# Sorted block attention into a gated MLP: the second batch's attention output turned by transposing transfers, all units in a new order, the last copy on two engines

## The chip, the core and the metric

The kernel runs on one core of a Trainium2 chip. The core has a matrix engine (TensorE, PE in the profile), a vector engine (VectorE, DVE), a scalar engine (ScalarE, ACT), a general engine (GpSimd, POOL) and a sequencer for transfers (SyncE, SP). SP, ACT and POOL issue transfers, which 16 DMA engines carry out. TensorE writes only to PSUM, eight banks of 128 partitions by 2 KB; VectorE and ScalarE copy results from there to the on-chip memory SBUF. The metric is the device time of one execution in microseconds; the median of several runs counts.

## The reference

Inputs are q, k, v (4 batches, 8 heads, 768 tokens, 64 per head) and sort_net (4, 8, 8, 8), and four weights of an MLP. First sorted block attention:

```python
P = sort_net
for _ in range(5):                       # Sinkhorn
    P = np.exp(P - np.max(P, axis=-1, keepdims=True))
    P = P / (np.sum(P, axis=-1, keepdims=True) + 1e-09)
    P = P / (np.sum(P, axis=-2, keepdims=True) + 1e-09)
k_sorted = np.einsum('bhij,bhjcd->bhicd', P, k_b)   # 8 blocks of 96 tokens, mixed by P
v_sorted = np.einsum('bhij,bhjcd->bhicd', P, v_b)
scores = scale * q_b @ k_sb.T            # each block attends to its own mixed block
attn = softmax(scores)
attn_out = attn @ v_sb                   # -> x: (4, 768, 512)
```

then a gated MLP with a spatial mix over the 768 tokens:

```python
h = np.maximum(x @ w_in, 0.0)            # 512 -> 1024
u, v = h[..., :512], h[..., 512:]
v_n = (v - mean) / sqrt(var + 1e-06)     # over the 512
v_s = np.einsum('ts,bsd->btd', w_spatial, v_n) + b_spatial[None, :, None]
out = (u * v_s) @ w_out                  # (4, 768, 512)
```

## The kernel before

Everything is cut into units, small functions `u_XX`, and one written list (`ORDER`) says in which order they are issued. An item such as `VP:14:D:0:3` calls `u_VP` with its arguments. Each engine works off its own instructions in the order in which the list issues them, and waits where a tile that it needs is not ready or a buffer not free; so the list sets the order on PE, DVE, ACT, POOL and on the queues of SP and ACT alike. Nothing is planned at run time.

PSUM is addressed by a number, the first argument of most units: 0 to 3 are pairs of banks, 10 to 17 the single banks, so 0 holds 10 and 11, 1 holds 12 and 13, 2 holds 14 and 15, 3 holds 16 and 17. A letter (A or D) names the engine that copies the result out. Then come the batch and the part of it: a head pair hp (four of them), a half ih of the blocks (two), a tile n of 128 tokens (six), a chunk mc of 128 gate columns (four).

The units, in the order in which a batch passes through them:

- `SK` (five times, at the start, for all batches): one Sinkhorn step on ACT and DVE; `PR`, `P0`, `PC`, `PD`: the mixing matrices pd, by PE and DVE for batch 0, by POOL for the others.
- `L`: a load, issued by POOL, which also casts to bf16; `LH`, `QC`: half of batch 0's q, loaded by ACT's queue as it is and cast on ACT.
- `QT` (and `QQ`, two head pairs at once): q turned on PE by 12 transposes, L324. In batch 3 `QP` reorders q and `QX` turns it by a transposing transfer.
- `KT`, `VT`: k or v mixed by pd on PE and turned at once, L393. `VB` turns v back by blocks, L411. For batches 1 to 3 `VM` mixes v on PE (L420) and `VC` distributes it by eight transfers (L433), which AT reads as vb.
- `SC`: scores of one head pair and half, PE L452, and their exponential on ACT, L457.
- `AT`: the attention output, PE L498, divided by the sums on DVE, L505 and L506, into the tile x.
- `XT`: x turned for the MLP: eight transposes on PE (L528) and a copy out of PSUM for one half and two head pairs. `XD`: the same for one half and all head pairs by a transposing transfer from SP, L516. Before the change batches 0 and 1 use XT, four units each, and batches 2 and 3 use XD, two each.
- `VP`: the v half of the first MLP matrix for one or two token tiles, PE L564, with ReLU on the way out. `ST`: its mean and variance on DVE, L581 and L582; `LN`: the inverse root on ACT; `LA`: the normalising on DVE, L593. `WT` (and `WW`, two at once): the spatial weight turned on PE.
- `UP`: the u half, PE L607. `SP`: the spatial mix of one chunk, PE L619, plus the bias on DVE into z, L625; it needs all six normalised tiles of its batch. `GT`: u times z, on POOL or DVE. `OP`, `OE`, `OS`: the last product (L645), its copy and its store.
- For the end of batch 3 `SH`, `GH`, `OH`, `OI`, `OJ` do the last four with smaller pieces.
- `DM`: matmuls on zeros at the start, as many as the second number, so that PE works before its data arrive. `CK`, `CF`, `LF`: whether the sums stayed in range; the branch at `IF` would otherwise recompute all by a general path, which does not run here.

Batches overlap: while PE does the MLP of one batch, it does the attention of the next between.

Of the kernel before, what the change touches and what calls it, by code (L numbers as in the profile page):

```python
# [34 lines left out]
VP:10:D:1:3 SC:1:2:3:0 SC:3:2:1:0 ST:1:0 GT:P:0:1 ST:1:4 QP:A:3:2 ST:1:3 UP:2:A:1:0:1 OP:0:0:2:2 ST:1:5 AT:1:2:2:1  # L35
OE:A:0:2 AT:3:2:3:0 OP:2:0:0:2 LN:1:0:6 LA:1:0 LA:1:5 LA:1:1 QP:A:3:3 OE:A:0:0 OP:0:0:4:2 OE:A:0:4 LA:1:4 LA:1:3
VM:1:A:3:3 VM:3:A:3:1 QP:A:3:0 LA:1:2 SP:2:1:0 XD:2:1 QX:3:0:4 VM:0:A:3:2 AT:1:2:0:0 SP:3:1:1 L:k:3:0:8 VM:2:D:3:0
AT:0:2:1:0 SP:1:1:3 OS:0:2:0:2 UP:3:A:1:1:1 VC:3:0:4 AT:2:2:2:0 KT:0:A:3:0 KT:1:D:3:1 XD:2:0 GT:P:1:3 KT:3:D:3:2
GT:P:1:1 KT:2:A:3:3 SP:0:1:2 SC:1:3:2:0 SC:2:3:2:1 VP:16:A:2:5 AT:0:3:2:0 VP:17:D:2:3 SC:1:3:3:0 SC:2:3:0:1 OS:0:4:0:2
ST:2:3 ST:2:5 SC:0:3:1:1 VP:16:D:2:4 VC:3:4:8:0:4 AT:1:3:3:0 VP:17:A:2:0 UP:2:A:2:1:1 AT:0:3:2:1 VP:16:D:2:2 ST:2:2  # L40
SC:1:3:0:0 ST:2:0 GT:P:1:0 SC:2:3:1:0 SC:0:3:3:1 ST:2:4 VP:17:A:2:1 UP:1:A:2:1:0 ST:2:1 UP:2:A:2:0:0 GT:P:1:2 LN:2:0:6
AT:0:3:3:1 OP:3:1:2:2 OE:A:1:2 LA:2:4 LA:2:3 AT:1:3:0:0 AT:2:3:1:1 LA:2:5 LA:2:2 OP:0:1:4:2 AT:3:3:1:0 AT:1:3:0:1
UP:2:A:2:0:1 LA:2:1 LA:2:0 OP:3:1:0:2 OE:A:1:4 XD:3:0 OS:0:0:0:2 XD:3:1 SP:1:2:2 SP:2:2:3 GT:D:2:3 SP:0:2:1 CK
SP:1:2:0 VP:10:A:3:1 VP:11:A:3:2 OE:D:1:0 VP:14:A:3:5 ST:3:5 VP:10:A:3:0 GT:D:2:0 OS:1:0:0:2:A UP:1:D:3:0:1 CF:11
GT:P:2:1 VP:10:D:3:3 GT:P:2:2 ST:3:3 UP:3:D:3:1:0 ST:3:0 ST:3:1 VP:11:A:3:4 ST:3:4 ST:3:2 LF OP:2:2:2:2 LN:3:0:6
LA:3:1 LA:3:2 UP:1:A:3:0:0 OE:A:2:2 LA:3:5 LA:3:3 OP:3:2:0:2 LA:3:0 LA:3:4 OP:0:2:4:2 OE:D:2:0 UP:1:D:3:1:1 OE:A:2:4
OS:1:2:0:2 SH:14:3:2:0 SH:15:3:3:0 GH:P:3:3:0 SH:14:3:0:0 GH:D:3:2:0 SH:15:3:1:0 GH:P:3:0:0 SH:14:3:1:1 SH:12:3:2:1
OS:2:4 GH:P:3:1:0 SH:15:3:3:1 OS:2:0 GH:D:3:1:1 SH:14:3:0:1 OS:1:4 GH:D:3:3:1 OS:2:2 GH:P:3:0:1 GH:P:3:2:1 IF
# [788 lines left out]
```

## Time and profile before

| | |
|---|---|
| time, median of 3 runs | 153.27 us (153.04 to 153.84) |
| the profiled execution | 154.13 us, span 152.3 us |
| PE busy | 143.7 us (94%) |
| DVE busy | 114.7 us (75%) |
| ACT busy | 85.0 us (56%) |
| POOL busy | 42.3 us (28%) |
| instructions | 4112 |
| moved by DMA | 24.38 MB |

The span is the time from the first to the last instruction in the trace of one execution; the profiled execution's own time lies 1.8 us above it and 0.86 us above the median of the runs. Busy time of PE counts matmuls whose ends are modelled, since they are pipelined. A group in the profile is a line, an engine, an operation and its shapes, with the number of instructions, their busy time in us, the mean duration of one in ns, and the engine's idle time just before them with what ended it. The chain of waits is followed back from the last instruction, at each step to what released it, or to the instruction before it on its engine. L123 and L121 are a helper, `copy`, on DVE and on ACT; L129 and L127 the same for ReLU.

### The profile page before, as it was taken

What the parts mean: (1) busy time and instruction counts of PE and PEld (TensorE: products, weight loads), DVE (VectorE), ACT (ScalarE), POOL (GpSimd) and SP (SyncE); (2) the same over time, 40 slices, a digit from 0 to 9 for tenths busy, and PEclk for the clock granted to TensorE, in tenths of its full rate; (3) what the DMA queues carried; (4) which work ended last, traced back from release to release, by engine and by line L of the source; (5) the groups of instructions that cost most, each with busy time, mean ns of one, the idle gap of its engine ahead of it and who ended that gap; (6) DMA issues with size and microseconds to landing.
All of it is one profiled execution on the core that took longest, in us unless ns stands there. A gap on an engine that the chain in (4) does not pass through costs nothing.

```text
span 152.3 us, 4112 instructions
## 1 busy us (share of the span) xinstructions
PE 143.7 (94%) x1687; PEld 95.9 (63%) x1687; DVE 114.7 (75%) x264; ACT 85.0 (56%) x122; POOL 42.3 (28%) x46
## 2 busy tenths in 40 slices
...
GB/s 102 255 204 204 185 190 205 208 214 237 240 257 205 204 185 8 118 127 197 202 163 75 230 218 285 69 0 4 0 223 126 0 108 167 0 50 403 115 189 229
DMA packets 30695, 24.38 MB, mean 160 GB/s; under 512 B 10384, under 2 KB 27792, under 8 KB 30672
## 3 DMA queue, kind: packets, MB, share of 16 engines
...
## 4 chain that ended last, share of the span: by engine, by line
PE 83%; DVE 10%; DMA 2%; issue 1%; ACT 1%; DVEq 0%
PE ps L619 15%; PE ps L564 14%; PE ps L607 14%; PE ps L645 10%; PE ps L675 5%; PE ps L498 5%; PE ps L452 4%; PE ps L393 4%; PE ps L695 3%; PE ps L420 3%; PE ps L528 2%; PE ps L324 2%; DVE x_sb L506 2%; DMA p_all<-in_sort_net_dram 2%; PE ps L411 1%
## 5 line engine op out<-in xcount | busy, mean ns | idle before, releaser
L636 POOL TENSOR_TENSOR gt<-z,u_sb 128x768 bf16<-128x768 f32 x9 | 14.6, 1637 | 70.1 <-DVE z L625 27.9
L457 ACT ACTIVATE ex_all<-ps 96x768 bf16<-96x768 f32 x32 | 23.9, 805 | 5.0 <-PE ps L452 4.6
L619 PE MATMUL ps<-wspT,v_sb 128*128 128x384 bf16 x144 | 24.9, 326 | 0.0
L564 PE MATMUL ps<-w_in_sb,xT 128*128 128x512 bf16 x96 | 23.4, 380 | 0.0
L607 PE MATMUL ps<-xT,w_in_sb 128*128 128x384 bf16 x128 | 23.1, 326 | 0.0
L506 DVE TENSOR_TENSOR x_sb<-ps,rec_all 96x512 bf16<-96x512 f32 x32 | 22.0, 686 | 1.1
L625 DVE TENSOR_TENSOR z<-ps,b_bc 128x768 f32<-128x768 f32 x12 | 11.4, 953 | 13.1 <-PE ps L619 13.1
L619 PEld LDWEIGHTS <-v_sb 128*128 128x128 bf16 x144 | 13.7, 98 | 8.7
L127 ACT ACTIVATE v_sb<-ps 128x512 bf16<-128x512 f32 (+1 forms) x15 | 9.9, 657 | 15.9 <-DVE bad L722 8.7
L581 DVE BATCH_NORM_STATS2 stats<-v_sb 128x6 f32<-128x512 bf16 x24 | 16.2, 674 | 1.7 <-ACT v_sb L127 1.5
L607 PEld LDWEIGHTS <-w_in_sb 128*128 128x128 bf16 x128 | 12.1, 98 | 7.9
L645 PE MATMUL ps<-w_out_sb,gt 128*128 128x256 bf16 x144 | 16.9, 273 | 0.0
L121 ACT COPY o_sb<-ps 128x1024 f32<-128x1024 f32 (+1 forms) x10 | 8.8, 882 | 12.9 <-DVE z L681 9.0
L127 ACT ACTIVATE u_sb<-ps 128x768 bf16<-128x768 f32 x12 | 9.7, 809 | 10.3 <-PE ps L607 10.3
L645 PEld LDWEIGHTS <-gt 128*128 128x128 bf16 x144 | 13.9, 98 | 2.1
L564 PEld LDWEIGHTS <-xT 128*128 128x128 bf16 x96 | 8.4, 98 | 8.5
L498 PEld LDWEIGHTS <-ex_all 96*128 96x128 bf16 x256 | 10.7, 97 | 3.6 <-issue 0.6
L498 PE MATMUL ps<-vb,ex_all 96*128 96x65 bf16 x256 | 11.8, 193 | 0.2 <-DVE x_sb L506 0.2
L291 POOL TENSOR_TENSOR pd<-mask,prep_sb 128x512 bf16<-128x512 bf16 x6 | 6.6, 1103 | 14.4 <-ACT prep_sb L121 9.6
L688 POOL TENSOR_TENSOR gt<-z,u_sb 128x512 bf16<-128x512 f32 (+1 forms) x5 | 5.2, 1046 | 18.4 <-DVE z L681 18.4
L121 ACT CAST vm<-ps 128x768 bf16<-128x768 f32 x9 | 7.1, 807 | 4.8 <-PE ps L420 4.7
L235 PE MATMUL ps<-warm 128*128 128x256 bf16 (+1 forms) x34 | 8.1, 400 | 1.3 <-DVE warm L209 1.3
...
## 6 DMA issues: line engine op xcount, KB each, us to landing
out_dram<-o_sb SPq DMA_DIRECT2D x8, 512.0 KB, 3.4
...
w_in_sb<-in_moe_w_in_dram POOLq DMA_DIRECT2D x2, 512.0 KB, 12.4
...
```

What stands on the lines that cost most here:

```text
L121: nc.scalar.copy(out=out, in_=in_)
L127: nc.scalar.activation(out=out, in_=in_, func=AF.Relu)
L457: nc.scalar.activation(out=e_tile(b, hp, ih).rearrange("p h (x g) -> p h x g", g=G), in_=t[0:BLK, :, 0:HW].rearrange("p h (g x) -> p h x g ...
L498: nc.tensor.matmul(t[:, hh, ii * VW:ii * VW + D + 1], lhsT=e[:, c:c + 128], rhs=vb[b % 2][:, ih * NI + ii, 2 * hp + hh, 0:D + 1], start=Tr ...
L506: nc.vector.tensor_mul(out=x_sb[:, hp].rearrange("p i (h d) -> p h i d", h=2), in0=tv[:, :, :, 0:D], in1=_raw_ap(rec, 0, [rec.ap[0], [NI, ...
L564: nc.tensor.matmul(t[:, x, :], lhsT=st["xT", b][:, n // 3, kc, (n % 3) * 128:(n % 3 + 1) * 128], rhs=w_in_sb[:, kc, DH:DFF], start=(kc == ...
L581: nc.vector.bn_stats(out=stats, in_=st["v_sb", b, n])
L607: nc.tensor.matmul(t[:, x, 0:HW], lhsT=w_in_sb[:, kc, mc * 128:(mc + 1) * 128], rhs=st["xT", b][:, ih, kc, :], start=(kc == 0), stop=(kc = ...
L619: nc.tensor.matmul(t[:, x, 0:HW], lhsT=st["v_sb", b, n][:, mc * 128:(mc + 1) * 128], rhs=wspT[:, 3 * x:3 * x + 3, n, :], start=(n == 0), s ...
L625: nc.vector.tensor_add(out=z.rearrange("p (x c) -> p x c", x=2), in0=t[:, :, 0:HW], in1=b_bc.rearrange("p (x c) -> p x c", x=2),)
L636: eng.tensor_mul(out=gt, in0=st["z", b, mc], in1=u)
L645: nc.tensor.matmul(t[:, x, c:c + w], lhsT=st["gt", b, mc][:, (n0 + x) * 128:(n0 + x + 1) * 128], rhs=w_out_sb[:, mc, c:c + w], start=(mc = ...
```

## The change

Three things change.

1. Batch 1's attention output x is turned by two XD units (`XD:1:1`, `XD:1:0`) where four XT units stood (`XT:12:D:1:0:2`, `XT:13:D:1:0:0`, `XT:10:D:1:1:0`, `XT:11:A:1:1:2`).
2. All units stand in a new order, with other banks and copying engines. At the front k of batch 0 is loaded and mixed before v, the scores of batch 0 begin before its v is mixed, the warm-up matmuls have 16,512 columns in all where they had 11,776, QQ is two QT, and all four q copies of batch 0 go to ACT (before: QQ and one QT on ACT, one on DVE); PC goes to DVE. Up to the first VP both lists hold the same work on PE and eleven scores each. Four of the six turned pieces of the spatial weight are copied by DVE, all by single WT units, where ACT copied all. Batch 0's VP units take one tile each, where two units took two. The loads of wu, the second half of the spatial weight and v of batch 2 are issued behind the first part of batch 2's pd on POOL, the load of q of batch 3, of w_out and of v of batch 3 behind gate products. Half of batch 2's VC goes through ACT's queue, and three OS where one did. For the last two tiles of batch 2 and all of batch 3 a new unit VH does what VP does with 256 columns to a matmul instead of 512.
3. The last `OI` of all (`OI:B`) copies one half of its 256 columns on ACT and the other on DVE.

```diff
 ORDER = """
-S0 CO DM:10:5:512 IV:0 LH:A:0 TB SK:0 DM:10:3:512 L:q:0:4:8 BH ID SK:1 SK:2 IV:2 QC:A:0 DM:10:4:512 QC:A:1 SK:3 MA
-L:v:0:0:8 MC SK:4 QQ:0:A:0:0 DM:12:10:256 DM:12:8:256 L:k:0:0:8 QT:12:D:0:3 PR:13 L:v:1:0:8 MB DM:10:4:256 P0:0:2
-P0:2:4 P0:4:6 P0:6:8 VT:2:A:0:0 PC:A VT:3:D:0:1 QT:12:A:0:2 VB:10:D:0:0 PD:1:0:4 VB:11:A:0:1 VT:2:D:0:3 L:k:1:0:8
-VT:3:A:0:2 KT:1:D:0:2 KT:0:A:0:0 KT:2:D:0:1 PD:1:4:8 KT:3:A:0:3 L:q:1:0:8 SC:1:0:2:1 VB:10:D:0:2 VB:11:D:0:3 L:wv L:wu
-SC:2:0:3:0 SC:3:0:3:1 L:wsb AT:1:0:2:1 SC:0:0:1:0 L:wsa AT:2:0:3:0 SC:1:0:0:0 AT:3:0:3:1 VM:0:A:1:1 AT:2:0:1:0
-SC:1:0:1:1 XT:16:D:0:1:2 VM:0:A:1:2 AT:2:0:0:0 SC:3:0:0:1 AT:1:0:1:1 SC:0:0:2:0 KT:2:D:1:1 KT:3:A:1:0 AT:1:0:0:1
-VM:0:D:1:0 VM:2:A:1:3 XT:16:A:0:0:0 AT:1:0:2:0 XT:17:D:0:1:0 KT:2:A:1:3 KT:0:A:1:2 QT:16:D:1:3 QT:12:D:1:0 QT:13:A:1:2
-L:v:2:0:8 QT:14:D:1:1 PD:2:4:8 XT:15:D:0:0:2 SC:3:1:0:0 BI SC:0:1:3:0 VC:1:0:4 SC:1:1:2:0 L:q:2:0:8 VP:14:D:0:3
-VP:3:A:0:0:2 ST:0:3 PD:3:4:8 ST:0:2 VP:0:A:0:1:5 ST:0:0 VP:16:D:0:4 PD:3:0:4 ST:0:4 SC:2:1:1:1 SC:1:1:1:0 UP:0:A:0:0:0
-ST:0:1 ST:0:5 L:k:2:0:8 UP:3:A:0:0:1 WW:2:A:4 AT:1:1:2:0 AT:0:1:0:0 LN:0:0:6 L:q:3:0:8 UP:3:A:0:1:0 LA:0:3 AT:1:1:3:0
-AT:2:1:1:0 LA:0:1 WW:0:A:2 UP:3:A:0:1:1 LA:0:4 XT:12:D:1:0:2 XT:13:D:1:0:0 VC:1:4:8 LA:0:2 SC:2:1:0:1 LA:0:0
-SC:0:1:2:1 SC:3:1:3:1 PD:2:0:4 WT:12:A:0 LA:0:5 WT:13:A:1 UP:2:D:1:1:0 VP:10:A:1:1 AT:3:1:1:1 VP:11:A:1:2 VM:2:D:2:1
-AT:1:1:3:1 VM:3:A:2:2 SP:0:0:2 AT:2:1:0:1 AT:3:1:2:1 SP:1:0:3 VM:0:A:2:3 UP:2:A:1:0:0 VM:3:A:2:0 SP:1:0:0 GT:P:0:3
-GT:P:0:0 KT:0:A:2:1 QT:16:D:2:0 QT:17:D:2:1 KT:2:A:2:2 KT:1:D:2:0 QT:10:A:2:3 QT:11:D:2:2 KT:3:A:2:3 L:wo QP:D:3:1
-ST:1:2 SC:2:2:1:1 SC:1:2:0:1 XT:10:D:1:1:0 XT:11:A:1:1:2 SP:3:0:1 SC:2:2:3:1 SC:1:2:0:0 VP:11:A:1:0 L:v:3:0:8 VC:2:4:8
-ST:1:1 AT:3:2:1:1 AT:2:2:0:1 VP:10:A:1:4 SC:1:2:2:0 GT:D:0:2 VC:2:0:4:0:4 SC:3:2:2:1 VP:11:A:1:5 AT:2:2:3:1
...
-OH:12:3:5:0:256:0:4 OI:D:3:5:0:256 OJ:3:1:0:512:S OJ:3:4:256:512:A OH:15:3:5:256:512:0:4 OJ:3:5:0:256:A
-OI:D:3:5:256:512 OH:14:3:4:0:256:0:4 OI:D:3:4:0:256 OJ:3:5:256:512:S OJ:3:4:0:256:A
+S0 CO L:q:0:4:8 DM:10:1:384 DM:10:6:384 LH:A:0 TB SK:0 BH ID SK:1 DM:10:7:512 SK:2 L:k:0:0:8 L:v:0:0:8 MC SK:3 QC:A:0
+MA DM:10:9:512 L:v:1:0:8 QC:A:1 SK:4 QT:10:A:0:2 QT:11:A:0:3 QT:12:A:0:0 DM:13:9:512 PR:10 MB P0:2:4 P0:4:6
+QT:11:A:0:1 L:k:1:0:8 P0:6:8 KT:2:A:0:1 P0:0:2 DM:13:2:512 KT:3:A:0:0 PC:D KT:1:D:0:2 SC:0:0:1:0 KT:2:D:0:3 IV:0
+SC:3:0:0:1 VT:1:A:0:0 VT:0:D:0:1 SC:2:0:3:0 SC:3:0:0:0 VB:12:D:0:0 VT:0:A:0:2 IV:2 VB:13:D:0:1 PD:1:0:4 SC:2:0:1:1
+AT:3:0:0:1 VT:0:A:0:3 AT:1:0:1:0 PD:1:4:8 VM:2:A:1:3 VM:3:D:1:1 SC:0:0:3:1 VB:12:D:0:2 VM:2:A:1:2 AT:3:0:1:1
+VM:0:A:1:0 VB:13:D:0:3 SC:2:0:2:0 AT:3:0:0:0 KT:0:A:1:2 AT:1:0:3:0 AT:2:0:2:0 SC:3:0:2:1 L:q:1:0:8 KT:0:A:1:0
+XT:12:D:0:0:0 L:wv L:wsa XT:13:A:0:1:0 AT:3:0:3:1 KT:2:A:1:1 AT:0:0:2:1 XT:12:D:0:0:2 KT:3:A:1:3 QT:13:A:1:2
+QT:14:D:1:1 QT:15:D:1:0 QT:10:D:1:3 PD:3:4:8 VC:1:0:4 XT:11:D:0:1:2 SC:3:1:1:0 SC:1:1:0:0 SC:2:1:2:0 VP:10:D:0:1 L:wu
+PD:2:0:4 VP:11:D:0:0 SC:3:1:0:1 SC:1:1:3:1 ST:0:1 L:wsb L:v:2:0:8 VP:10:A:0:4 AT:2:1:1:0 AT:3:1:2:0 VP:11:A:0:3
+AT:1:1:0:0 WT:10:A:0 ST:0:0 PD:2:4:8 ST:0:4 VP:14:A:0:2 SC:3:1:3:0 SC:0:1:2:1 SC:1:1:1:1 WT:15:D:2 ST:0:2 ST:0:3
+VP:14:A:0:5 ST:0:5 UP:3:A:0:1:0 LN:0:0:6 AT:0:1:3:0 UP:1:A:0:0:1 LA:0:2 LA:0:4 UP:2:A:0:0:0 LA:0:5 PD:3:0:4 LA:0:3
+VC:1:4:8 WT:10:A:5 LA:0:1 WT:11:D:3 WT:12:D:1 WT:13:D:4 BI LA:0:0 AT:3:1:0:1 L:k:2:0:8 AT:2:1:1:1 L:q:2:0:8
+UP:0:A:0:1:1 SP:1:0:0 AT:3:1:3:1 AT:0:1:2:1 SP:2:0:1 VM:1:A:2:3 VM:3:D:2:2 SP:0:0:3 VM:2:A:2:0 XD:1:1 VM:1:A:2:1
+GT:D:0:0 GT:P:0:3 SP:3:0:2 VC:2:4:8:0:4:A KT:0:A:2:2 QT:12:D:2:3 L:q:3:0:8 GT:P:0:2 QT:13:D:2:0 KT:2:A:2:3 KT:3:D:2:1
+QT:12:D:2:2 XD:1:0 QT:13:D:2:1 KT:0:A:2:0 VP:14:D:1:2 SC:3:2:2:1 SC:0:2:3:1 L:wo SC:1:2:0:1 VP:15:A:1:3 L:v:3:0:8
+AT:3:2:2:1 VP:14:D:1:4 VP:10:D:1:1 SC:3:2:2:0 SC:1:2:0:0 SC:2:2:1:1 QP:A:3:0 VP:11:D:1:5 UP:3:A:1:1:1 VC:2:0:4:0:4
+ST:1:5 AT:1:2:3:1 AT:0:2:0:1 UP:2:A:1:0:0 GT:P:0:1 AT:1:2:0:0 VP:16:A:1:0 SC:0:2:3:0 ST:1:3 ST:1:0 QP:A:3:2 ST:1:1
+SC:2:2:1:0 OP:1:0:0:2 ST:1:4 ST:1:2 OE:A:0:0 LN:1:0:6 OP:3:0:2:2 OE:A:0:2 OS:0:2:0:2 AT:0:2:1:0 L:k:3:0:8 AT:2:2:1:1
+LA:1:4 UP:1:D:1:1:0 AT:0:2:3:0 VM:3:A:3:0 UP:2:A:1:0:1 LA:1:0 LA:1:2 LA:1:3 OS:0:0:0:2:A LA:1:5 LA:1:1 VM:3:A:3:1
...
+LA:2:3 OS:1:0:0:2:A UP:2:A:2:0:1 OP:1:1:2:2 LA:2:1 LA:2:4 AT:0:3:1:1 AT:3:3:0:1 SP:2:2:2 XD:3:1 AT:0:3:0:0 AT:3:3:2:0
+GT:D:2:2 CK OE:A:1:2 OP:1:1:4:2 SP:2:2:1 SP:0:2:0 OS:0:4:0:2:A XD:3:0 SP:3:2:3 CF:10 VH:11:D:3:3 VH:2:A:3:4:5 GT:D:2:0
...
+OH:12:3:4:256:512:0:4 OI:D:3:4:256:512 OH:10:3:5:0:256:0:4 OI:D:3:5:0:256 OJ:3:1:0:512:S OJ:3:4:256:512:A
+OH:11:3:5:256:512:0:4 OJ:3:5:0:256:A OI:D:3:5:256:512 OH:13:3:4:0:256:0:4 OI:B:3:4:0:256 OJ:3:5:256:512:S
+OJ:3:4:0:256:A
 """
...
                 nc.tensor.transpose(t[:, k // 2, k % 2, i, :], st["x", b, ih][:, k, i, :], ident[0:BLK, 0:BLK])
         copy(eng, st["xT", b][:, ih].rearrange("p (x k) c -> p x (k c)", x=2), tt)
 
-    def u_VP(ps, eng, b, *tiles):
+    def u_VP(ps, eng, b, *tiles, parts=1):
         b = int(b)
         t = ps_tile(ps)
         nt = len(tiles)
         for x, n in enumerate(tiles):
             n = int(n)
-            for kc in range(KC):
-                nc.tensor.matmul(
-                    t[:, x, :],
-                    lhsT=st["xT", b][:, n // 3, kc, (n % 3) * 128:(n % 3 + 1) * 128],
-                    rhs=w_in_sb[:, kc, DH:DFF],
-                    start=(kc == 0), stop=(kc == KC - 1),
-                )
+            for c in range(0, DH, DH // parts):
+                for kc in range(KC):
+                    nc.tensor.matmul(
+                        t[:, x, c:c + DH // parts],
+                        lhsT=st["xT", b][:, n // 3, kc, (n % 3) * 128:(n % 3 + 1) * 128],
+                        rhs=w_in_sb[:, kc, DH + c:DH + c + DH // parts],
+                        start=(kc == 0), stop=(kc == KC - 1),
+                    )
         v_sb = moe.tile([128, 2, DH], BF16, name="v_sb", tag="v", bufs=6)
         relu(eng, v_sb[:, 0:nt], t[:, 0:nt])
         for x, n in enumerate(tiles):
             st["v_sb", b, int(n)] = v_sb[:, x, :]
+
+    def u_VH(ps, eng, b, *tiles):
+        u_VP(ps, eng, b, *tiles, parts=2)
 
     def u_ST(b, n):
         b, n = int(b), int(n)
     def u_OI(eng, b, n, c0, c1):
         b, n, c0, c1 = (int(x) for x in (b, n, c0, c1))
         st["o1", b, n, c0] = ld.tile([128, 3, DM], FP32, name="o1_sb", tag="ld")[:, 0, 0:c1 - c0]
-        copy(eng, st["o1", b, n, c0], st["o1_ps", b, n, c0])
+        o, of = st["o1", b, n, c0], st["o1_ps", b, n, c0]
+        if eng == "B":
+            half = (c1 - c0) // 2
+            copy("A", o[:, 0:half], of[:, 0:half])
+            copy("D", o[:, half:], of[:, half:])
+        else:
+            copy(eng, o, of)
 
     def u_OJ(b, n, c0, c1, eng="S"):
         b, n, c0, c1 = (int(x) for x in (b, n, c0, c1))
```

27 lines of the change are left out of this document (11 added, 16 removed).

## The prediction

> **What bounds the kernel now.** I read the page's first part, then the chain of waits, then the busy time by stretches, and last the groups and the transfers. The page gives each engine's busy time and its share of the span, and the chain's shares by engine:
>
> ```profile
> PE 143.7 (94%) x1687; PEld 95.9 (63%) x1687; DVE 114.7 (75%) x264; ACT 85.0 (56%) x122; POOL 42.3 (28%) x46
> ...
> PE 83%; DVE 10%; DMA 2%; issue 1%; ACT 1%; DVEq 0%
> ```
>
> TensorE (PE) is busy nearly throughout and carries most of the chain. The stretches (start:end, length, then busy time of PE, weight loads, DVE, ACT and POOL) say where it is not:
>
> ```profile
> 13.00:33.00 20.00, 18.26 (x431) 14.85 (x429) 18.11 (x35) 16.93 (x24) 13.10 (x15) 1.00 1.27 199
> ...
> 33.00:149.00 116.00, 115.92 (x1191) 76.00 (x1183) 88.22 (x189) 62.20 (x89) 24.61 (x20) 1.00 0.69 149
> ```
>
> From 33 to 149 us PE idles 0.08 us, at full clock. There every microsecond taken from PE is a microsecond of the result, and every new wait of PE is one too. From 13 to 33 DVE, with 18.11 of 20 us, is as full as PE. The chain in order of time (start, length, what) shows the joints:
>
> ```profile
> 12.35 0.44 DVE qT L123
> ...
> 12.98 0.43 DVE pd L279
> ...
> 33.18 5.29 PE ps L564 x24
> ...
> 46.57 0.68 PE ps L528 x16
> ...
> 64.35 0.79 PE ps L528 x16
> ...
> 149.01 0.42 DVE o_sb L123
> ```
>
> A copy of turned q stands on the chain before the mixing matrices (pd) are built. The first VP starts at 33.18, and from there the chain is PE up to the last copy at 149.01. The two pieces of L528 at 46.57 and 64.35 are the second batch's XT units, 32 transposes.
>
> **The change, part by part.** The sum is made against the profiled execution (154.13 us, span 152.3), which is 0.86 above the median of 153.27; I apply differences to the median.
>
> *Transposes off PE.* The four XT of batch 1 are 0.68 + 0.79 = **1.47 us** of PE, both pieces in the full stretch. Nothing of that work is left on PE, so the term is -1.47. Their four copies go too (three on DVE, one on ACT). In their place SP issues two transposes:
>
> ```profile
> xT<-x_sb SPq DMA_TRANSPOSE x4, 4.0
> ```
> ```profile
> L516 SPq DMA_TRANSPOSE xT<-x_sb x4: 1441/1507/2272, 77.3 to 112.3; - x4
> ```
> ```profile
> L433 SPq DMA_DIRECT2D vb<-vm x24: 571/598/770, 29.5 to 94.5; - x24
> ...
> DMA to landing us min/median/max: 2.7/4.4/8.5
> ```
>
> They take SP 1.44 to 2.27 us to issue and land after 4.0 us (median). The third fence is the vb<-vm transfers of VC: 0.6 us an issue, landed after 2.7 us in an empty queue, 8.5 beside the early loads. To be hidden, the second transpose (XD:1:0) must land before VP:14:D:1:2. Count from the start S of SP:1:0:0, with these pieces of the chain:
>
> ```profile
> 30.14 1.36 PE ps L324 x48
> ...
> 38.91 2.71 PE ps L607 x16
> ...
> 41.62 0.67 PE ps L541 x12
> ...
> 52.81 1.95 PE ps L619 x12
> 54.77 0.48 PE ps L498 x16
> ...
> 79.95 0.65 PE ps L420 x4
> ...
> 89.14 1.54 PE ps L393 x48
> ```
>
> and these groups (busy, mean ns):
>
> ```profile
> L506 DVE TENSOR_TENSOR x_sb<-ps,rec_all 96x512 bf16<-96x512 f32 x32 | 22.0, 686 | 1.1
> L581 DVE BATCH_NORM_STATS2 stats<-v_sb 128x6 f32<-128x512 bf16 x24 | 16.2, 674 | 1.7 <-ACT v_sb L127 1.5
> ...
> L625 DVE TENSOR_TENSOR z<-ps,b_bc 128x768 f32<-128x768 f32 x12 | 11.4, 953 | 13.1 <-PE ps L619 13.1
> ...
> L593 DVE TENSOR_SCALAR v_sb<-v_sb,mv,rstd 128x512 bf16<-128x512 bf16 x24 | 8.4, 405 | 0.7 <-ACT rstd L588 0.6
> ...
> L505 DVE RECIPROCAL rec_all<-ps 96x8 f32<-96x8 f32 x32 | 6.3, 196 | 3.6 <-PE ps L498 3.0 <-PE ps L452 0.4
> ...
> L129 DVE TENSOR_SCALAR v_sb<-ps 128x512 bf16<-128x512 f32 x7 | 4.8, 679 | 1.0 <-PE ps L564 1.0
> ...
> L582 DVE BATCH_NORM_AGGREGATE mv<-stats 128x2 f32<-128x6 f32 x24 | 4.4, 182 | 0.8
> ```
>
> PE from S to that VP: four SP 7.80, two AT 0.48, four VM 1.30, four KT 1.54, four QT 1.36: 12.5 us. DVE: SP:1 ends at S+1.95, its z takes 0.95, the two last AT 0.88 each (0.196 + 0.686), so the last row of x stands at about S+4.7. XD:1:1 issues until S+6.2 to S+7.0, and XD:1:0 lands 4.0 later: S+10.2 to S+11.0. Slack 1.5 to 2.3 us, cost **0**; the cover is batch 2's SP, KT and QT work. Without it the whole 4.0 would show. Behind the two on SP stands only half of batch 2's VC (0.6 us an issue), which its first AT of that half needs more than ten units later.
>
> By the Trainium skill, page "DMA: Bandwidth & Descriptors", section "Queues, rings and completion order", each DMA engine takes turns between the queues that have work, a packet at a time. By that rule a transpose beside a busy load queue gets about half, lands after some 8 us (an estimate from the 4.0), and PE would wait 1.7 to 2.5 us, where the row alone gives 0. The trace agrees in kind: 2.7 against 8.5 for one kind of transfer.
>
> *The front, up to the first VP.* Both orders hold the same PE units before it, as many scores, so its start is compared directly. What moves is who copies, by these groups:
>
> ```profile
> L121 ACT CAST kt_all<-ps 128x768 bf16<-128x768 f32 x10 | 7.9, 801 | 1.8 <-PE ps L393 1.7
> ...
> L123 DVE CAST kt_all<-ps 128x768 bf16<-128x768 f32 x6 | 5.5, 946 | 0.0
> ...
> L123 DVE COPY qT<-ps 128x768 bf16<-128x768 bf16 x7 | 3.6, 542 | 0.0
> ...
> L121 ACT COPY qT<-ps 128x768 bf16<-128x768 bf16 x3 | 2.4, 814 | 0.0
> ...
> L123 DVE COPY vb<-ps 96x1024 bf16<-96x1024 bf16 x3 | 2.0, 684 | 0.5 <-PE ps L411 0.5
> ...
> L121 ACT COPY qT<-ps 128x1536 bf16<-128x1536 bf16 x1 | 1.4, 1411 | 0.0
> ...
> L121 ACT COPY vb<-ps 96x1024 bf16<-96x1024 bf16 x1 | 1.0, 1008 | 0.2 <-PE ps L411 0.2
> ...
> L121 ACT CAST prep_sb<-ps 128x256 bf16<-128x256 f32 x1 | 0.4, 378 | 0.0
> ```
>
> DVE loses one KT, one VT and one QT copy (0.946 twice, the VT cast having the KT cast's shape, and 0.542) and gets one VB and PC (0.684 + about 0.38): **-1.4 us**. ACT gets one KT, one VT and three QT (0.80 + 0.80 + 2.44) and loses QQ, VB and PC (1.41 + 1.01 + 0.38): +1.2, which fits into the 3.07 us that it idled from 13 to 33. The q copy of 0.44 leaves the chain before pd; against it, both QC copies now run between the fourth and the fifth Sinkhorn exponential, and may hold the fifth a little. Since k is loaded and mixed before v, the scores' exponentials start sooner. Before, the last Sinkhorn exponential and the first of a score stood here:
>
> ```profile
> 10.35 0.26 ACT L247 ACTIVATE p_all<-p_all 32x64 f32<-32x64 f32 x1 [1.00 <-DVE p_all L258]
> ...
> 19.16 0.81 ACT L457 ACTIVATE ex_all<-ps 96x768 bf16<-96x768 f32 x1
> ```
>
> After, ACT has four q copies and two KT copies (3.26 + 1.60) between the two, so the first score's follows at 15.5 or a little later, over 3 us sooner, and ACT need not idle. Bounds: the first VP cannot run before the v half of w_in has landed, with the same bytes ahead of it:
>
> ```profile
> 19.15 0.76 POOL L181 DMA_DIRECT2D w_in_sb<-in_moe_w_in_dram  x1
> ```
> ```profile
> w_in_sb<-in_moe_w_in_dram POOLq DMA_DIRECT2D x1, 512.0 KB, 11.5
> ```
>
> That is 30.65, at best -2.5. At worst ACT, now as full as DVE, passes its lateness through the shared PSUM banks: +1.0. I take **-1.0**, two thirds of DVE's relief. More warm-up columns (16,512 against 11,776) lie under the Sinkhorn chain: 0 while they end before pd; running over is part of the +1.0.
>
> *Waits of PE after 33 us.* DVE has less before the first VP and more behind it: four of the six WT copies, two more VP evacuations. Before SP:1:0:0 it owes two evacuations (1.36), six ST (5.14), four AT (3.53), four WT copies (2.17, priced as qT copies) and six LA (2.43): 14.6, beginning 1.1 us after the first VP starts. PE's cover is six VP 5.29, four UP 5.42, six WT 2.01, six AT 1.44, five scores, taken a little under an AT, 1.1: 15.3. So DVE is 0.4 late by busy sums and on time if neighbours overlap a little. Two orders that fill PE to 0.08 us bound this from below at 0; above, two such stages with DVE idling 1 us in each: 2.5. I take **+0.7**, nearer the row of 0.08. VH splits eight tiles' matmuls at 256 columns: same columns, 0. WT for WW and single-tile VP: same matmuls, 0 on PE. VC for half the heads' rows of batch 2 and two OS go to ACT's queue: four times 0.6 us that block ACT behind batch 2's last VM copy; behind them waits KT:0:A:2:2's copy, covered by SP:3:0:2, three KT and four QT before the bank is wanted (1.95 + 1.16 + 1.36 = 4.5 us, against a VM copy, the issues and the KT copy, 0.8 + 2.4 + 0.8 = 4.0): 0. The loads of wu, wsb and v2 are issued later on POOL, behind pd of batch 2, but their queue was full: 0. L:q:3, wo and v:3 now stand behind gate products, 2 us ahead of use by my count: 0, and 1 to 2 late if not.
>
> *The last copy.* 256 columns shared by ACT and DVE instead of 0.42 on DVE: between 0 and -0.21, **-0.1**.
>
> Sum: -1.47 - 1.0 + 0.7 - 0.1 = **-1.87**; 153.27 - 1.87 = **151.4 us**.
>
> **The rivals.**
> *DVE binds.* Speaking for it: the 0.4 above, and DVE full in the same stretches as PE. Against: DVE is busy 88.22 of 116 us. If two normalising stages lose 1.5 us each in place of the 0.7: -1.87 + 2.3, **153.7**; if one, **152.2**; middle 153.0, no measurable change.
> *The front gains nothing* because ACT takes over as its bound: -0.87, **152.4**.
> *A late transpose* ends on the other side. Place: VP:14:D:1:2. For it: loads slow vb<-vm from 2.7 to 8.5. Against: the transfers' share (the last column but one of the stretches) falls from 1.27 before 33 us to a mean of 0.69 after it. If landing takes 4.0 times 2.1 to 3.1 (5.7 being about the middle of 2.7 and 8.5), that is 8.4 to 12.6 us, a stall of 2.1 to 6.9: 153.6 to 158.4, middle about **155**. It makes the kernel slower by over 0.5% (0.77 us, about what a measurement can tell from none) once the stall passes 2.64, a landing after some 8.5 us. The Trainium skill's turn-taking rule, as worked out above, would end just short of that point.
>
> **How the numbers follow.** Forecast 0.55 (own range 150.4 to 152.4); DVE binds 0.2; front gains nothing 0.1; late transpose 0.15. Faster by over 0.5%: forecast, most of the front case, a little of DVE: 0.63. Within 0.5%: most of DVE: 0.2. Slower: late transpose and the end of DVE: 0.17. The range runs from the front's full gain with no waits (153.27 - 1.47 - 2.0, rounded) to a modest late transpose: 149.8 to 154.3.
>
> **What the profile after would show.** No L528-type piece of the chain between 40 and 70; two transposes more on SP's queue, landing in 4 to 5 us. The first VP at 31 to 33. DVE lighter than ACT from 13 to 33. PE idle under 1 us from the first VP to the end, its waits short and named after DVE. The forecast is wrong if PE waits over 2 us in one place: for v_sb L593 before the first SP, for xT before VP:14, or for a load.

## The result and the profile after

The changed kernel is slower: 156.64 us (median of 154.76, 155.84, 157.45 and 157.49) against 153.18 for the kernel before in the same series. The ratio, 1.0123 with a 95% interval of 1.0087 to 1.0158, leaves out the two longest of these executions (the profiled one below is one of them), whose mean granted clock was 0.987 and 0.985 where the other two, 155.3 us in the mean, show 1.00. The forecast was 151.4 us, faster; the time lies outside the stated range of 149.8 to 154.3 too.

The profiled execution took 157.49 us, span 155.7. The page's busy times and chain of waits, by engine and by line:

```profile
PE 145.8 (94%) x1687; PEld 97.6 (63%) x1687; DVE 118.4 (76%) x270; ACT 80.0 (51%) x118; POOL 42.7 (27%) x45
...
PE 55%; DMA 5%; ACTq 1%; DVE 0%; issue 0%; ACT 0%
PE ps L566 10%; PE ps L650 10%; PE ps L612 10%; PE ps L624 10%; PE ps L680 5%; DMA vb<-vm 5%; PE ps L700 3%; PE ps L499 3%; PE ps L453 2%; ACTq L434 1%; PE ps L394 1%; PE ps L421 1%; DVE o_sb L124 0%; ACT o_sb L122 0%; PE ps L746 0%
```

A transfer, vb<-vm, now has 5% of the chain. (L434 is VC, L499 AT, L566 VP, L394 KT, L517 XD, L680 SH, L700 OH, L122 and L124 the copy on ACT and DVE. In the kernel before, L675 is SH and L695 OH.) The stretches, with the same columns as before, place the loss:

```profile
13.00:33.00 20.00, 18.81 (x418) 14.47 (x413) 16.64 (x33) 17.60 (x25) 10.61 (x12) 1.00 1.27 214
33.00:53.00 20.00, 20.00 (x226) 12.97 (x225) 18.37 (x43) 12.64 (x20) 3.02 (x4) 1.00 1.21 214
53.00:65.00 12.00, 9.94 (x154) 6.47 (x153) 6.77 (x10) 6.36 (x9) 8.94 (x7) 1.00 0.97 184
65.00:66.00 1.00, 0.19 (x1) 0.10 (x1) 0.00 (x0) 0.05 (x1) 0.00 (x0) 1.00 1.29 200
66.00:68.00 2.00, 1.93 (x10) 0.82 (x10) 0.89 (x2) 0.00 (x0) 0.00 (x0) 0.57 1.25 206
68.00:70.00 2.00, 2.00 (x19) 0.60 (x19) 0.81 (x2) 0.00 (x0) 0.00 (x0) 0.58 1.30 204
71.00:151.00 80.00, 80.00 (x753) 55.54 (x752) 64.93 (x137) 35.14 (x51) 14.64 (x10) 1.00 0.48 121
```

PE is full up to 53 us and from 71 us on. From 53 to 66 it idles 2.06 + 0.81 = 2.9 us, and from 66 to 70 its granted clock is 0.57 to 0.58. What stands there is in the timeline (start, busy time, instruction; in brackets the engine's idle time before it and what ended that):

```profile
56.11 2.84 SPq L434 DMA_DIRECT2D vb<-vm  x4
56.16 3.20 ACTq L434 DMA_DIRECT2D vb<-vm  x4
...
57.54 0.94 POOL L177 DMA_DIRECT2D q_in<-in_q_dram  x1
...
59.46 2.21 ACT L122 CAST kt_all<-ps 128x768 bf16<-128x768 f32 x3 [3.38 <-PE ps L394]
...
65.28 0.19 PE L499 MATMUL ps<-vb,ex_all 96*128 96x65 bf16 x1 [1.60 <-DMA vb<-vm]
...
66.07 0.31 PE L499 MATMUL ps<-vb,ex_all 96*128 96x65 bf16 x5 [0.60 <-DMA vb<-vm]
66.22 3.55 PE L566 MATMUL ps<-w_in_sb,xT 128*128 128x512 bf16 x8
```

and in the transfers issued from 55 to 60 us (queue, number, size, median us to landing):

```profile
q_in<-in_q_dram POOLq DMA_DIRECT2D x1, 768.0 KB, 10.3
vb<-vm SPq DMA_DIRECT2D x4, 99.0 KB, 3.7
vb<-vm ACTq DMA_DIRECT2D x4, 99.0 KB, 5.4
xT<-x_sb SPq DMA_TRANSPOSE x1, 3.7
```

Both halves of batch 2's VC go out at 56.1 us, one on SP, one on ACT. Into them falls L:q:3, the load of batch 3's q, which POOL issues at 57.54 when the gate product ahead of it is done. AT:3:2:2:1 reads the half on ACT's queue; PE waits for it 1.60 and 0.60 us, and then runs eight VP matmuls in 3.39 us on the chain, twice the 1.73 that two tiles take elsewhere (0.86 and 0.87 in the rows of before). The chain has it in three lines:

```profile
58.49 7.54 DMA vb<-vm
...
66.07 0.31 PE ps L499 x5
66.38 3.39 PE ps L566 x8
```

The fourth transfer on ACT's queue took 7.54 us. The turned x of batch 1 landed after 3.7 us, and no VP waited for it.

### The profile page after: what moved, and what is told of

It reads as the page before. It is cut to its first block, busy times and chain, and to the rows that moved or that the text cites. A ratio compares the mean times of both kernels' runs of the same rounds, so it can differ in the third digit from the quotient of the medians.

```text
span 155.7 us, 4105 instructions
## 1 busy us (share of the span) xinstructions
PE 145.8 (94%) x1687; PEld 97.6 (63%) x1687; DVE 118.4 (76%) x270; ACT 80.0 (51%) x118; POOL 42.7 (27%) x45
## 4 chain that ended last, share of the span: by engine, by line
PE 55%; DMA 5%; ACTq 1%; DVE 0%; issue 0%; ACT 0%
PE ps L566 10%; PE ps L650 10%; PE ps L612 10%; PE ps L624 10%; PE ps L680 5%; DMA vb<-vm 5%; PE ps L700 3%; PE ps L499 3%; PE ps L453 2%; ACTq L434 1%; PE ps L394 1%; PE ps L421 1%; DVE o_sb L124 0%; ACT o_sb L122 0%; PE ps L746 0%
## 5 line engine op out<-in xcount | busy, mean ns | idle before, releaser
L566 PE MATMUL ps<-w_in_sb,xT 128*128 128x512 bf16 (+1 forms) x128 | 25.2, 342 | 0.2 <-ACT kt_all L122 0.2
L122 ACT COPY o_sb<-ps 128x1024 f32<-128x1024 f32 (+2 forms) x11 | 9.1, 825 | 17.5 <-DVE z L686 10.7
L566 PEld LDWEIGHTS <-xT 128*128 128x128 bf16 x128 | 11.8, 100 | 7.1 <-issue 1.8
L128 ACT ACTIVATE v_sb<-ps 128x512 bf16<-128x512 f32 (+1 forms) x12 | 7.5, 635 | 14.1 <-PE ps L566 14.0
L499 PE MATMUL ps<-vb,ex_all 96*128 96x65 bf16 x256 | 11.9, 193 | 2.2 <-DMA vb<-vm 2.2
L122 ACT CAST kt_all<-ps 128x768 bf16<-128x768 f32 x11 | 8.5, 801 | 10.2 <-PE ps L394 10.0
L499 PEld LDWEIGHTS <-ex_all 96*128 96x128 bf16 x256 | 10.5, 97 | 4.9 <-issue 2.5
L130 DVE TENSOR_SCALAR v_sb<-ps 128x512 bf16<-128x512 f32 x11 | 7.5, 686 | 5.4 <-PE ps L566 5.4
L122 ACT CAST vm<-ps 128x768 bf16<-128x768 f32 x9 | 7.0, 803 | 8.5 <-PE ps L421 8.5
```

Of the source, the lines that this page charges most:

```text
L122: nc.scalar.copy(out=out, in_=in_)
L128: nc.scalar.activation(out=out, in_=in_, func=AF.Relu)
L499: nc.tensor.matmul(t[:, hh, ii * VW:ii * VW + D + 1], lhsT=e[:, c:c + 128], rhs=vb[b % 2][:, ih * NI + ii, 2 * hp + hh, 0:D + 1], start=Tr ...
L566: nc.tensor.matmul(t[:, x, c:c + DH // parts], lhsT=st["xT", b][:, n // 3, kc, (n % 3) * 128:(n % 3 + 1) * 128], rhs=w_in_sb[:, kc, DH + c ...
```

## The experiments

Times are medians; "before" is the kernel before in the same series (153.2 to 153.5 us).

**VC on SP alone, and the load earlier.** The first series undid the two suspects, singly and together, and kept PE busy through the wait. In e1 all of VC goes to SP, with XD:1:0 ahead of it; in e2 only the load moves, so that it should be over before VC:

```diff
 e1
-XD:1:1 VM:1:A:2:1
-VC:2:4:8:0:4:A
-QT:12:D:2:2 XD:1:0 QT:13:D:2:1
+XD:1:1 XD:1:0 VM:1:A:2:1
+VC:2:4:8
+QT:12:D:2:2 QT:13:D:2:1
 e2
-AT:2:1:1:1 L:q:2:0:8
-QT:12:D:2:3 L:q:3:0:8 GT:P:0:2
+AT:2:1:1:1 L:q:2:0:8 L:q:3:0:8
+QT:12:D:2:3 GT:P:0:2
 e3: e1 and e2 together
 e4
-AT:3:2:2:1
+DM:11:12:512 AT:3:2:2:1
```

> Edit: the four transfers of VC:2:4:8 go through SP's queue instead of ACT's, behind the two transposes (XD:1:0 moved ahead of them) and ahead of VC:2:0:4. Theory A (the place of the loss is these four transfers: issued by ACT from 56.2 to 59.4 beside four others from SP, they block ACT for 3.2 us and the last lands 7.5 us after its issue, so AT:3:2:2:1 waits): the four are issued by 58.5 alone, the last lands before 62 to 63, PE's wait on vb falls under 1 us, the clock stays full there, ACT copies KT at once; 151.4 to 152.6. Rival B (the load of q of batch 3, issued at 57.5, slows whatever vb transfers are in flight, on either queue): the wait stays over 1.5 us; above 154. Rival C (DVE or the new order elsewhere holds PE): no change in time, 155 to 157.

> Edit: only the load of q of batch 3 is moved, from between the gate products (57.5 us) to right behind the load of q of batch 2 (36 us). The vb transfers stay on ACT's queue. Theory A (queue and issue on ACT): ACT is blocked as before, the last of the four is issued at 59.4 and lands 3 to 4 us later instead of 7.5; the wait shrinks to under 1 us but about 1 us of PE idle from the late KT copies stays; 152.5 to 153.5. Rival B (the load alone): 151.4 to 152.3. If neither, the weights of w_out and v of batch 3, issued from 60.3 on, slow the last transfer anyway: wait over 1.5 us, above 154.

> Edit: both moves together. Theory A and rival B both expect the wait on vb gone and PE full from the first VP to the end as before the change: 151.4, between 151.0 and 152.2. If the order has other waits (rival C), it stays above 153.

> Edit: the changed kernel, with twelve matmuls on zeros of 512 columns (about 2.6 us) put on PE right ahead of AT:3:2:2:1, where it waits for vb. The wait for the transfers stays. If half of the loss is the clock, which the trace shows at 0.50 from 66 to 70 us behind the wait, the slow runs go: every run between 154.4 and 155.2. If the clock does not depend on the idle time, the runs spread as those of the changed kernel, 154.8 to 157.5.

e1 took 153.25 us (ratio 0.9985, 0.9971 to 0.9998), e2 154.24 (1.0056, 1.0038 to 1.0073), e3 158.41 (1.0349, 1.0312 to 1.0386), e4 156.12 (1.0176, 1.0150 to 1.0201). So either edit alone takes back 2.4 to 3.4 us of the changed kernel's median (1.1 to 2.1 against the 155.3 of the two shorter executions). Both together, where its first two theories had expected 151.4, lose more than the change did. PE's waits in e3 from 32 to 100 us (us in total, times, longest) and, from its timeline between 50 and 60 us, what SP issued:

```profile
PE ps L499 <- DMA vb<-vm: 3.1, 2, 3.0
PE ps L566 <- DMA xT<-x_sb: 0.4, 1, 0.4
```
```profile
51.58 6.81 SPq L517 DMA_TRANSPOSE xT<-x_sb  x2
58.50 1.93 SPq L434 DMA_DIRECT2D vb<-vm  x3
```

With the load at its earlier place the two XD run beside it. They hold SP for 6.81 us (3.33 in the changed kernel) and land after a median of 6.7; VC behind them on SP starts only at 58.50 and now meets the load of w_out. In e2 VC's half on ACT's queue was not behind the XD: it went out at 55.9, and PE hardly waited for vb; it waited 0.6 us for xT and 1.0 for a KT copy instead, so e2's time lies where its third expectation put it, above 154, but not for the reason given there. In the changed kernel, e2 and e3 the load stretched whatever transfers ran beside it. In e1, with the load at its place in the changed kernel and all of VC on SP, this much of the wait is left:

```profile
PE ps L499 <- DMA vb<-vm: 0.3, 1, 0.3
```

The Trainium skill, page "DMA: Bandwidth & Descriptors", section "Queues, rings and completion order", has each DMA engine take turns between queues; the trace agrees in kind, with 3.7 us for a transpose alone and 6.7 to 7.4 beside a load (an estimate from that rule was 8).

e4's twelve idle matmuls kept the clock: 1.00 from 66 to 70 us, and its four times lie within 0.33 us, where the changed kernel's spread over 2.7. So the half clock is a consequence of PE's wait, as far as four executions of each kernel show it. It accounts for 1.7 us of that spread (3.39 - 1.73): 157.49 less 1.7 is about the 155.84 of another execution; why the lowest took 154.76 no profile shows. e4 lay above the 154.4 to 155.2 expected. Its idle matmuls cover the wait and don't shorten it: they begin at 63.67 us and take 2.75, to 66.4, when in the changed kernel the last transfer had landed at 66.0 (58.49 + 7.54). e1 lay 0.6 to 1.9 us above what was expected of it.

**Which of the two, the load or the queue?** e8 takes the load away from VC to the other side, behind k's, and leaves half of VC on ACT; e12 leaves the load and swaps VC's two halves between the queues; e13 puts w_out's load (512 KB) where q's stood and moves a copy of q behind it.

```diff
 e8
-QT:12:D:2:3 L:q:3:0:8 GT:P:0:2
-QP:A:3:0 VP:11:D:1:5
-ST:1:0 QP:A:3:2 ST:1:1
-AT:0:2:1:0 L:k:3:0:8
-XD:2:1 QP:A:3:3
+QT:12:D:2:3 GT:P:0:2
+VP:11:D:1:5
+ST:1:0 ST:1:1
+AT:0:2:1:0 L:k:3:0:8 L:q:3:0:8
+XD:2:1 QP:A:3:0 QP:A:3:2 QP:A:3:3
 e12 (with XD:1:0 moved as in e1)
-VC:2:4:8:0:4:A
-UP:3:A:1:1:1 VC:2:0:4:0:4
+VC:2:4:8 VC:2:0:4:0:4:A
+UP:3:A:1:1:1
 e13 (on e6, below)
-QT:12:D:2:3 L:q:3:0:8 GT:P:0:2
-SC:0:2:3:1 L:wo SC:1:2:0:1
-VP:16:A:1:0 QP:A:3:0 SC:0:2:3:0
-OE:A:0:2 OS:0:2:0:2
+QT:12:D:2:3 L:wo GT:P:0:2
+SC:0:2:3:1 L:q:3:0:8 SC:1:2:0:1
+VP:16:A:1:0 SC:0:2:3:0
+OE:A:0:2 QP:A:3:0 OS:0:2:0:2
```

> The changed kernel, with the load of batch 3's q behind that of k instead of ahead of w_out's, and its two ACT copies (QP:A:3:0, QP:A:3:2) moved behind XD:2:1. Batch 2's eight vb<-vm transfers still go out on ACT's and SP's queue at the same time, and ACT is blocked by its four. Theory A, the load is what stretches their landing (2.9 to 7.5 us): they land in 3 to 4 us, PE's wait for vb is under 0.5, the clock stays at 1.00, and 154.0 to 154.8 us remain for the blocked ACT. Theory B, the two queues hold each other up: the wait for vb stays over 1.5 us and the time at 156 or more.

> The changed kernel with the two queues swapped: the half of batch 2's VC that AT:3:2:2:1 reads first on SP (behind both XD), the other half on ACT in its old place, so ACT is blocked as long as in the changed kernel and as many transfers run at once beside the same load. Theory A, the first half lands later on ACT's queue than it would on SP's: PE's wait for vb falls under 0.7 us and the time to 154.0 to 154.8 (the rest is the blocked ACT). Theory B, any queue gets its share alike and only the number of transfers beside the load counts: the wait for vb stays at 1.5 us or more, 155.5 to 157.5 us.

> The best run so far (152.64 us: VC on SP, undivided last copy, q copy later) with the loads of w_out and of batch 3's q exchanged, and QP:A:3:0 behind OE:A:0:2, since PE waited 0.4 us at 71.5 for w_out. Theory A, the wait goes and nothing replaces it: 152.2 us (152.0 to 152.5). Theory B, the q that now comes later, or the smaller load beside vb, moves the wait: 152.6 us or more.

e8 took 153.08 us (0.9984, 0.9969 to 0.9999), below the 154.0 that its first theory expected at least. One load and two copies of what it brings moved, and 3.6 us of the median are gone with ACT's queue as it was (2.2 against 155.3, which is the wait's 2.2). The transfers that e8 issued from 55 to 60 us, and its stretches where PE had waited:

```profile
w_out_sb<-in_moe_w_out_dram POOLq DMA_DIRECT2D x1, 512.0 KB, 6.0
vb<-vm SPq DMA_DIRECT2D x4, 99.0 KB, 3.3
vb<-vm ACTq DMA_DIRECT2D x4, 99.0 KB, 3.3
```
```profile
58.00:62.00 4.00, 3.46 (x76) 2.43 (x75) 3.27 (x7) 2.35 (x4) 3.72 (x4) 1.00 0.69 185
62.00:66.00 4.00, 4.00 (x54) 2.09 (x49) 2.52 (x5) 3.14 (x5) 3.00 (x3) 1.00 1.19 171
```

On ACT's queue 5.4 us became 3.3, and the wait for vb is gone; 0.54 us of idle time are left. e12 took 154.69 (1.0101, 1.0076 to 1.0126) and e13 154.09 (1.0078, 1.0045 to 1.0111), with these waits of PE (us in total, times, longest), e12's first, then e13's:

```profile
PE ps L499 <- DMA vb<-vm: 1.3, 1, 1.3
```
```profile
PE ps L499 <- DMA vb<-vm: 1.3, 1, 1.3
```

So with the eight transfers at once beside the load PE waits 1.3 us even where the half that it needs goes out on SP (2.2 on ACT); in e1, where the other half goes out behind it on SP, 0.3. Neither of e12's theories is right alone. Of the 2.2 us some 0.9 hang on the queue of the half that is needed first (beside the load the half on ACT's queue landed after 5.2 us in e12, that on SP after 3.5), 1.0 on sending the other half at the same time, and all of it on the load, since without it the wait is gone (e8). And it needs no q: e13 has all of VC on SP like e6, which shows no wait for vb, and w_out's load brings the wait back. After these two waits of 1.3 us the clock stayed at 1.00 from 66 to 70 us in the profile, though one of e13's seven executions had a mean clock of 0.987. After 2.2 in the changed kernel and 3.0 in e3 it fell to 0.50 to 0.58.

**The transposes.** e7 puts the four XT of batch 1 back into the new order (on e5, below); e10 does the opposite, one transfer for half of batch 1 in the order of before; e11 adds 16 small warm-up matmuls to e10.

```diff
 e7
-XD:1:1 XD:1:0 VM:1:A:2:1
-QT:12:D:2:2 QT:13:D:2:1 KT:0:A:2:0 VP:14:D:1:2
-SC:1:2:0:1 VP:15:A:1:3
+VM:1:A:2:1
+QT:12:D:2:2 QT:13:D:2:1 XT:14:D:1:0:0 KT:0:A:2:0 XT:15:D:1:0:2 VP:14:D:1:2
+SC:1:2:0:1 XT:10:A:1:1:0 XT:11:D:1:1:2 VP:15:A:1:3
 e10, in the order of before
-AT:3:1:2:1 SP:1:0:3
-XT:10:D:1:1:0 XT:11:A:1:1:2 SP:3:0:1
+AT:3:1:2:1 XD:1:1 SP:1:0:3
+SP:3:0:1
 e11: e10, and
-QC:A:0 DM:10:4:512
+QC:A:0 DM:10:4:512 DM:10:16:64
```

> As the run with the undivided last copy, but batch 1 is turned by four XT units on PE again, ahead of the VP units that need them, and no XD of batch 1. Theory A, the two transposing transfers save PE their whole 1.47 us and nothing else hangs on them: 154.4 us (154.1 to 154.8). Theory B, PE waits at 58 to 66 us for copies and transfers anyway and the transposes would fill that idle time (0.74 us there): 153.7 us or less.

> The kernel before with one part of the change alone: the half ih 1 of batch 1 is turned by XD:1:1, issued behind AT:3:1:2:1, in place of XT:10:D:1:1:0 and XT:11:A:1:1:2 (0.79 us of PE on the chain at 64.35). Theory A, the transfer is hidden and PE's time falls by what it gave up: 0.79 us under the kernel before (0.6 to 0.9), about 152.7 us. Theory B, the transfer delays VC of batch 2 behind it on SP and the first AT of batch 2 waits: no gain, or a loss up to 1 us.

> The kernel before with XD:1:1 for half of batch 1, as already run (154.82 us), plus 16 warm-up matmuls of 64 columns behind DM:10:4:512, where PE idled 1.5 us. That run's PE stood 0.82 us for nothing that its profile names between the last SH and the first OH, just behind the branch. Theory A, this hangs on the number of PE instructions ahead of the branch (16 transposes fewer), so with as many as before the gap goes and the time is 153.1 to 154.1 us. Theory B, it has to do with the transfer itself or its place: the gap stays, 154.7 to 154.9 us.

e7 took 157.45 us (two of its four executions with a mean clock of 0.987), 4.6 more than e5 and outside both expectations. Up to its first SH it is 138.26 - 134.60 = 3.7 us behind e5, more than the 1.47 of the transposes, and its waits from 33 us on hold the rest:

```profile
PE ps L529 <- ACT ex_all L458: 1.3, 1, 1.3
PE ps L566 <- DVE xT L124: 0.6, 1, 0.6
PE ps L566 <- ACT xT L122: 0.6, 1, 0.6
PE ps L394 <- DVE z L630: 0.3, 1, 0.3
```

A transpose on PE also needs a bank and a copy on DVE or ACT; here, where the order had no room for them, that cost more than PE's own time. e10 took 154.82 us (1.0097, 1.0081 to 1.0113), against 152.7 expected, though the transfer was hidden. Two things ate the gain. From its first VP to its first SH it needs 102.70 us, the kernel before 102.82 (e15, below): of the 0.79 us given up 0.12 are left; PE now stands 0.5 us for a KT copy on ACT that the transposes had covered. And behind the branch (the list's `IF`, ahead of the first OH) stands a pause that nothing in the profile explains. e10's waits of PE from 33 us on, then its chain:

```profile
PE ps L695 <- issue: 0.8, 1, 0.8
PE ps L619 <- ACT kt_all L121: 0.5, 1, 0.5
```
```profile
135.00 7.80 PE ps L675 x48
142.80 0.82 issue
143.62 5.39 PE ps L695 x32
```

e11 was to test whether that hangs on the number of PE instructions. It took 154.08 us (1.0049, 1.0028 to 1.0071): PE's pause at that place is gone, but DVE stands 2.2 us ahead of its first output copy there, 2.4 in e10. The profile names for it only a load of k that had landed long before; in the kernel before DVE stands 1.4 us at this place, for PE. What the pause is, and whether the length of the code moves it, stays open.

**The last copy and the late q.** e5 is e1 with the last copy undivided; e6 also moves a copy of q.

```diff
 e5
-OI:B:3:4:0:256
+OI:D:3:4:0:256
 e6: e5, and
-QP:A:3:0 VP:11:D:1:5
-VP:16:A:1:0 SC:0:2:3:0
+VP:11:D:1:5
+VP:16:A:1:0 QP:A:3:0 SC:0:2:3:0
```

> As the run with VC on SP's queue (153.25 us), with the last copy undivided on DVE again (OI:D for OI:B). Theory A, the halves run one after the other: in that run ACT's half took 0.27 us from 147.93 and DVE's 0.29 from 148.23, 0.45 us after DVE was free; an undivided copy of 0.43 from 147.77 ends 0.3 us sooner. A expects 152.95 us (152.8 to 153.1), and the last copy 0.45 to 0.5 us behind the end of the copy ahead of it on DVE. Theory B, the prediction's: dividing saves 0.1, so this run takes 153.35 us.

> As the run with the undivided last copy, and QP:A:3:0 moved behind VP:16:A:1:0, since the load of batch 3's q landed only at 68.7 us and ACT waited 0.9 us for it ahead of UP:3:A:1:1:1's copy. Theory A, that wait reaches PE: 0.2 to 0.4 us less, 152.6 us (152.4 to 152.8), PE idle from 66 to 72 us under 0.1. Theory B, ACT's lateness only moves to the exponentials behind it: 152.95 us, with the same idle time of PE under another name.

e5 took 152.85 us (0.9966, 0.9952 to 0.9979), e6 152.64 (0.9961, 0.9948 to 0.9975). The undivided copy saves about the 0.3 expected (0.9985 to 0.9966 here, 0.9984 to 0.9964 from e8 to e14 below), though the intervals overlap. In the changed kernel the chain has one half behind the other, not beside it:

```profile
151.45 0.44 DVE o_sb L124
...
152.04 0.27 ACT o_sb L122
...
152.34 0.29 DVE o_sb L124
```

ACT's half starts 0.15 us after DVE is free, since ACT has a store to issue first. DVE's half then waits 0.46 us, and the timeline names the end of ACT's half as what releases it. e6's gain over e5 is within the scatter; ACT's wait of 1.0 us for q is gone, and PE waits 0.4 us for w_out instead.

**VC's queue once the load is away.** Both have the load late and the last copy whole; e9 has VC on SP, e14 half of it on ACT.

```diff
 e14: e8, and
-OI:B:3:4:0:256
+OI:D:3:4:0:256
 e9: e14, and
-XD:1:1 VM:1:A:2:1
-VC:2:4:8:0:4:A
-QT:12:D:2:2 XD:1:0 QT:13:D:2:1
+XD:1:1 XD:1:0 VM:1:A:2:1
+VC:2:4:8
+QT:12:D:2:2 QT:13:D:2:1
```

> The changed kernel with the load of batch 3's q behind that of k (and its two ACT copies later), the last copy undivided, and all of batch 2's VC on SP behind both XD. Against the next run, which differs in VC's queue alone. Theory A, a blocked ACT still costs PE what it idled at 58 to 62 us in the run with q late (0.54 us, of which 0.34 was for z): this one is 0.2 us faster than the next, 152.55 us (152.3 to 152.8). Theory B, VC's queue is indifferent once the load is away: both take the same, 152.8 us.

> The same with half of VC on ACT as in the changed kernel: 0.3 us under the run with q late (153.08), for the undivided last copy, so 152.8 us (152.6 to 153.0).

e9 took 152.97 us (0.9986, 0.9964 to 1.0007; 152.22 to 153.86), e14 152.73 (0.9964, 0.9947 to 0.9980; 152.52 to 152.99). No gain from SP, so B: without the load beside it, VC on ACT makes no difference that these times show. The Trainium skill, page "DMA: Bandwidth & Descriptors", section "Issuing engines are not separate DMA queues", says that issuing from several engines saves only the sequencer's time; that agrees with e9 and e14. e14 and e6 are faster than both kernels, by 0.4% against before.

**The kernel before again.** No edit.

> The kernel before, unchanged, for a second profile. Theory A, in the first profile the load of sort_net landed 0.7 us late (ACT waited 0.73 us for it ahead of the first Sinkhorn exponential), and this is the 0.86 us by which that execution lay above the median: here the first exponential starts at 2.6 us, the first VP at 32.2 to 32.5 and the span is 151.3 to 151.7 us. Theory B, the first VP at 33.2 is this kernel's usual one, and the 0.86 us lie elsewhere.

It took 153.37 us, span 151.6. The first Sinkhorn exponential and the first VP, in the timeline of the first profile of before:

```profile
3.31 0.26 ACT L247 ACTIVATE p_all<-p_all 32x64 f32<-32x64 f32 x1 [0.73 <-DMA p_all<-in_sort_net_dram]
...
33.11 3.19 PE L564 MATMUL ps<-w_in_sb,xT 128*128 128x512 bf16 x14
```

and of the second:

```profile
2.59 0.26 ACT L247 ACTIVATE p_all<-p_all 32x64 f32<-32x64 f32 x1
...
32.29 4.06 PE L564 MATMUL ps<-w_in_sb,xT 128*128 128x512 bf16 x17
```

In the first profile the 8 KB load of sort_net landed after 2.5 us, in the second after 1.8; the exponential starts 0.7 us later in the first than in the second, and the first VP 0.8. e10 and e11, with the order of before up to there (e11 with its 16 small matmuls more), start the first VP at 32.30 and 32.14; in all profiles of the new order it starts at 31.46 to 31.96.

## Why the prediction was wrong

Against the second profile of before, the changed kernel's 4.1 us of span come as -0.35 up to the first VP (31.94 against 32.29), +4.09 from there to the first SH (106.91 against 102.82), +0.27 to the end of the last copy (13.78 against 13.51), and +0.1 behind it.

- *The step that failed* is the pair "VC for half the heads' rows of batch 2 ... 0" and "L:q:3, wo and v:3 now stand behind gate products, 2 us ahead of use by my count: 0, and 1 to 2 late if not". Each was priced by itself and nearly right by itself: with the load away, VC on ACT costs about nothing (e14 against e9), and ACT waited 0.9 us for q in e1. Their meeting was not asked for. The load starts at 57.5 in the middle of eight vb<-vm transfers, and PE pays 2.2 us of waiting and, in the profiled execution, 1.7 of half clock. Moving that load gives back 3.6 us of the median (e8). No term and no rival had the clock. The prediction's sign of being wrong came true, over 2 us of waiting in one place, but for a tile that it did not list.
- *The late transpose*, the rival on the other side, had the mechanism (loads stretch vb<-vm from 2.7 to 8.5) but the wrong victim, so that its time, 153.6 to 158.4, holds the result by luck. (Its working gives 153.5 for the lower end, 151.4 + 2.1, and the 2.7 was not in an empty queue but beside a store, with no load.) The transposes were hidden as forecast. Beside a load they do land after 6.7 to 7.4 us, and in e2 and e3 PE waited only 0.4 to 0.6 for them.
- *Transposes off PE, -1.47*: mis-sized. e8, with the half clock and the wait for vb gone, needs 102.62 us from first VP (31.56) to first SH (134.18), 0.2 less than before, and e9 0.5 less. Adding up the time from each matmul's start to the next one's by unit, between first VP and first SH, tells where the 1.47 went: KT and QT take 5.61 us in e8 and 4.35 in the first profile of before (+1.26), VP with VH 21.66 and 21.28 (+0.4, where the prediction had 0 for VH), all else 0.4 less. What grew are batch 2's KT and QT. In before's chain they run without a gap until SC at 63.90; in e8 they last from 56.37 until VP can start at 60.52:

```profile
61.10 0.46 PE ps L393 x12
...
63.57 0.33 PE ps L393 x12
63.90 0.45 PE ps L452 x16
```
```profile
55.78 3.08 ACTq L434 DMA_DIRECT2D vb<-vm  x4
...
56.37 0.53 PE L394 MATMUL ps<-pd,k_in 128*64 128x128 bf16 x12
...
58.97 2.21 ACT L122 CAST kt_all<-ps 128x768 bf16<-128x768 f32 x3 [3.26 <-PE ps L394]
...
60.52 0.81 PE L566 MATMUL ps<-w_in_sb,xT 128*128 128x512 bf16 x3 [0.17 <-ACT kt_all L122]
```

That is 4.15 us where 2.80 stood. The trace names waits of 0.3 us for DVE's z and 0.2 for a KT copy on ACT there, and nothing for the other gaps. ACT's copies begin only when its four issues are done, which take 3.08 us (3.20 in the changed kernel) where the prediction had 2.4. With VC on SP (e9) KT and QT still take 5.06. e10 shows the same kind: a transpose taken away uncovers a copy that it hid.
- *The front, -1.0*: mis-sized at its root. The profile that it was worked out from had the late load in its first 3 us, and the working put the whole 0.86 us of that execution aside as if spread evenly. Against that profile the first VP starts 1.2 us sooner (31.94 against 33.11), against the second 0.35, and over all profiles of the new order 0.3 to 0.8. DVE's relief is there (18.11 to 16.64 us from 13 to 33) but ACT rose to 17.60, which is the rival "the front gains nothing" in part.
- *Waits of PE after 33 us, +0.7*: the wrong place. PE is full from 33 to 53 us, and no wait is named after L598, the normalising, so that the price taken for DVE was not paid. The waits amid KT and QT, which the sum had at 0, cost more than that price (the 1.26 above); that one stands in for part of the other is luck.
- *The last copy, -0.1*: wrong in sign; e5 puts it at +0.4 (153.25 against 152.85, in different series), the ratios and the chain at +0.3.
